# A small matmul moved next to its use, and two pieces of attention spaced evenly, in a kernel of attention and a Fourier mixer

## The chip, the core and the metric

The kernel runs on one core of a Trainium2 chip. Its engines work side by side, each in the order of its own instruction list: TensorE (PE, matmuls into PSUM; its weight loads are shown as PEld), VectorE (DVE), ScalarE (ACT), GpSimd (POOL), and SyncE (SP), which issues nearly all DMA transfers here. Engines wait for one another by semaphores. The metric is the device time of one execution in microseconds (us).

## The reference, cut

```python
q, k, v: (4, 8, 768, 64)            # batch, heads, tokens, head size
# attention: a window of +-16 tokens, and 24 blocks of 32 tokens as extra keys
k_sum = k.reshape(B, H, nb, block, D).max(axis=3)
v_sum = v.reshape(B, H, nb, block, D).mean(axis=3)
scores_l = scale * q @ k.T           # masked to |pos_i - pos_j| < 16
scores_s = scale * q @ k_sum.T + np.log(block)
a = softmax(concat[scores_l, scores_s])
x = a @ concat[v, v_sum]             # then (B, S, H*D) = (4, 768, 512)
# mixer
u  = x + np.real(fft(fft(x, axis=1), axis=2))
un = (u - mean(u)) / sqrt(var(u) + 1e-6)
out = u + relu(un @ w_ch1) @ w_ch2   # 512 -> 2048 -> 512
```

A block's log(32) and mean make a sum: the weight exp(score) times the sum of the block's 32 rows of v. The kernel therefore uses block *sums* of v and a count of 32.

## The kernel before

Four batches go through a pipeline. The dense work of batch b (two layers, 512 to 2048 to 512, each split in halves and done by seven products in place of eight) runs on TensorE together with the attention of batch b+1. Two Python generators are advanced side by side: `gen_hidden` and `gen_out` yield after every product or two, `gen_attention` after every small piece, and `drive` at the end of `_main_program` mixes them at a fixed ratio. For the attention of batches 2 and 3 it is 80 steps of attention on 44 of dense work. What is emitted between two yields is handed to a scheduler together; it sets each engine's order by its own model. So the number of yields between two pieces of attention sets how much dense work lies between them.

A batch's eight heads are four pairs g = 0..3. For a pair of batches 1 to 3:

- `prepare(b, g)` makes kt and qt, the transposed k and q, and km, the block maxima of k. In batches 2 and 3 (past pair 0 of batch 2) DVE transposes (line 693, `STREAM_TRANSPOSE`), in the rest PE does.
- `scores` (lines 773 and 779): 48 small products into two PSUM banks, exp on ACT into p, a multiplication by the mask near on DVE. `sum_scores` (lines 789 and 790): the scores of the blocks, exp into pm.
- `block_sums(b, gg)` fetches the v rows of four heads in four pieces of 192 KB and adds them up on POOL (line 570) to vbs, once for pairs 0 and 1 and once for pairs 2 and 3.
- `scale_sums` (lines 795 and 798) is the block sums' product: PE multiplies vbs with a 0/1 table that spreads the sums over the partitions, and two ACT copies (in batch 1 one DVE operation) write them, masked by half_of, into the single tile vs.
- `values` (lines 811 and 816): 48 products of p with the near values vw, then six of pm with vs, into the same two banks (av); a reciprocal (line 820) and a multiplication on DVE write x.
- `load` fetches q and k of the pair three ahead, `load_values` the near values vw, of the next pair.

The attention's PSUM banks are four in turn, the dense work's another four. In the hidden layer, slice j has seven groups of two matmuls in the order hx, hy, hx, hz, hx, hz, hx (line 1316); a matmul in fp32 shows as two records in the profile. Between the products that use one bank, ACT copies it (lines 1327, 1333, 1335 and 1346) or DVE adds it (line 567). Line 1385 has the products of the output layer (ox, oy, oz).

In `gen_attention` before, a pair of batches 2 and 3 goes: scores, three yields, k's transposition for the next pair, `scale_sums`, two yields, q's transposition, `load`, two yields, `values` and `load_values`, three yields, and the next pair's scores. That is seven steps from scores to values and three from values to scores.

## Time and profile before

| what | us |
|---|---|
| median of three runs | 809.16 (806.12 to 811.9) |
| the profiled execution | 806.47 |
| its span, first to last instruction | 804.5 |
| ACT busy in the span | 229.0 |
| stage with batch 2's attention (282.17 to 382.79): length | 100.62 |
| the same, PE busy | 95.95 |
| the near products of a pair, start to start of its second part (305.81 to 306.94) | 1.13 |

The profile covers one execution; times in it are counted from its first instruction. "PE busy" joins the modelled ends of pipelined matmuls. PEclk is the share of TensorE's full clock that was granted. A row of the timeline gives start, duration, engine, line, operation, the tiles written and read, the shapes and the count, and in brackets the engine's idle time before it with what ended it. Line numbers are those of the kernel before.

### The profile page before, as it was taken

How to read it: one execution, taken by the hardware profiler on the slowest of the kernel's cores; microseconds unless marked ns; L12 is line 12 of the kernel's file. 1: busy time of each engine (PE TensorE's matmuls, PEld its weight loads, DVE VectorE, ACT ScalarE, POOL GpSimd, SP SyncE). 2: the span in 40 equal slices, each digit the busy share in tenths (PEclk: the TensorE clock that was granted, in tenths of full speed). 3: DMA queues.
4: the chain of work that ended last, by engine and by line, in shares of the span. 5: the costliest groups of instructions: out<-in, count | busy, mean ns of one | idle time of the engine just before them, and what ended most of it. 6: DMA issues, size and time to landing. Idle time of an engine off the chain costs nothing.

```text
span 804.5 us, 14469 instructions
## 1 busy us (share of the span) xinstructions
PE 777.9 (97%) x5914; PEld 564.7 (70%) x5914; DVE 494.8 (62%) x1115; ACT 229.0 (28%) x509; POOL 61.7 (8%) x103
## 2 busy tenths in 40 slices
PE   8988999999999979999999999999999999999997
PEld 6776655445589846688669865688669875786586
DVE  5789998797988526653576635563476722532352
ACT  3544656336535122200126112200126102001200
POOL 0012030000000020200120010300030000000000
PEclk9989999999999999999999999999999999999999
DMA  9999597696855279965353159620514143205001
GB/s 228 202 271 193 148 311 187 196 311 204 231 159 141 51 198 237 238 89 133 120 191 138 53 185 185 175 90 11 228 42 152 40 176 144 86 0 229 0 28 55
DMA packets 133354, 121.83 MB, mean 151 GB/s; under 512 B 94464, under 2 KB 114912, under 8 KB 133088
## 3 DMA queue, kind: packets, MB, share of 16 engines
q1 hardware_dynamic: 132016, 118.53, 53.3%
q0 software_dynamic: 576, 2.10, 0.7%
q8 instruction: 48, 0.79, 0.4%
q10 hardware_dynamic: 688, 0.20, 0.1%
q14 instruction: 26, 0.21, 0.1%
HBM read 97.22 MB, written 23.59 MB: 150 GB/s over the span
## 4 chain that ended last, share of the span: by engine, by line
PE 81%; DVE 11%; DMA 3%; ACT 3%; POOL 1%; issue 1%; SPq 0%; ACTq 0%; POOLq 0%; DVEq 0%
PE ox L1385 18%; PE hx L1316 17%; PE oz L1385 9%; PE hz L1316 8%; PE oy L1385 5%; PE o L1362 4%; PE hy L1316 4%; PE y L1212 4%; PE mx L1171 2%; DMA vb<-in_v_dram 2%; DVE w L567 2%; PE av L811 1%; PE unt L1290 1%; PE sc L773 1%; DVE x L567 1%; PE av L816 1%
## 5 line engine op out<-in xcount | busy, mean ns | idle before, releaser
L1316 PE MATMUL hx<-u,w 128*128 128x384 f32 x512 | 187.0, 493 | 4.2 <-DVE h L567 2.9
L1316 PEld LDWEIGHTS hx<-u,w 128*128 128x128 f32 x512 | 95.0, 190 | 72.0 <-DVE h L567 5.3
L1316 PE MATMUL hz<-u,w 128*128 128x384 f32 x256 | 93.3, 486 | 0.0
L1385 PE MATMUL oz<-w,s 128*128 128x256 f32 x336 | 81.1, 379 | 0.0
L1385 PE MATMUL ox<-w,s 128*128 128x256 f32 x336 | 80.3, 380 | 0.0
L1385 PE MATMUL ox<-w,h 128*128 128x256 f32 x336 | 80.2, 381 | 0.0
L567 DVE TENSOR_TENSOR x<-ox,x 128x256 f32<-128x256 f32 x84 | 35.3, 422 | 67.6 <-PE ox L1385 67.4
L1316 PEld LDWEIGHTS hz<-u,w 128*128 128x128 f32 x256 | 48.5, 190 | 34.3 <-ACT h L1335 1.2
L1327 ACT COPY h<-hx 128x384 f32<-128x384 f32 x32 | 15.3, 478 | 199.8 <-PE hx L1316 199.8
L1385 PEld LDWEIGHTS ox<-w,h 128*128 128x128 f32 x336 | 62.9, 190 | 10.4 <-issue 0.6
L1385 PEld LDWEIGHTS ox<-w,s 128*128 128x128 f32 x336 | 63.0, 190 | 9.3 <-DVE x L567 0.8
L1385 PEld LDWEIGHTS oz<-w,s 128*128 128x128 f32 x336 | 63.4, 190 | 8.5
L567 DVE TENSOR_TENSOR h<-hy,h 128x384 f32<-128x384 f32 x32 | 17.8, 555 | 55.9 <-PE hy L1316 55.8
L1316 PE MATMUL hy<-u,w 128*128 128x384 f32 x128 | 47.4, 494 | 0.0
L567 DVE TENSOR_TENSOR h<-hx,h 128x384 f32<-128x384 f32 x32 | 17.7, 555 | 47.3 <-PE hx L1316 46.5
L1362 PE MATMUL o<-w,h 128*128 128x512 f32 x96 | 42.2, 596 | 0.7 <-DVE w L567 0.7
L1346 ACT ACTIVATE h<-hx 128x384 f32<-128x384 f32 x32 | 15.7, 491 | 86.5 <-PE hx L1316 86.4
L1385 PE MATMUL oy<-w,h 128*128 128x256 f32 x168 | 40.1, 380 | 0.0
L1316 PEld LDWEIGHTS hy<-u,w 128*128 128x128 f32 x128 | 24.8, 194 | 17.4 <-issue 1.2
L570 POOL TENSOR_TENSOR vb<-vb 96x512 f32<-96x512 f32 (+2 forms) x24 | 23.6, 984 | 174.6 <-PE hz L1316 66.2
L567 DVE TENSOR_TENSOR x<-oz,x 128x256 f32<-128x256 f32 x42 | 17.7, 422 | 29.7 <-PE oz L1385 29.4
L1385 PEld LDWEIGHTS oy<-w,h 128*128 128x128 f32 x168 | 31.8, 190 | 4.4
(164 smaller groups left out, 1093.8 us busy)
## 6 DMA issues: line engine op xcount, KB each, us to landing
w<-dw SPq DMA_DIRECT2D x44, 896.0 KB, 5.6
words<-in_moe_w_ch_dram SPq DMA_DIRECT2D x32, 512.0 KB, 5.1
dw<-w SPq DMA_DIRECT2D x12, 896.0 KB, 7.1
vw<-in_v_dram SPq DMA_DIRECT2D x47, 192.0 KB, 5.4
out_dram<-x SPq DMA_DIRECT2D x23, 256.0 KB, 2.0
vb<-in_v_dram SPq DMA_DIRECT2D x24, 192.0 KB, 6.3
kn<-in_k_dram SPq DMA_DIRECT2D x9, 384.0 KB, 5.2
qn<-in_q_dram SPq DMA_DIRECT2D x9, 384.0 KB, 6.7
```

The costliest lines, as they stand in the source:

```text
L567: return nc.vector.tensor_tensor(out=out, in0=in0, in1=in1, op=op).ins
L570: nc.gpsimd.tensor_tensor(out=out, in0=in0, in1=in1, op=op)
L773: nc.tensor.matmul(ps[h][r:r + 64, i, :], kt[rows, o:o + 64], qt[rows, o:o + BLOCK], start=True, stop=True)
L811: nc.tensor.matmul(av[r][32 * j:32 * (j + 1), t, :], p[rows, h, i - NB2 * h, :], vw[rows, i, :], start=(t == 0), stop=False, skip_group_ch ...
L816: nc.tensor.matmul(av[r][:, t:t + HT + 1:HT, :], pm[rows, P * t:P * (t + 1)], vs[rows], start=False, stop=(t == HT - 1), skip_group_check= ...
L1171: nc.tensor.matmul(out, y[:, g], table, start=False, stop=True, skip_group_check=True)
L1212: nc.tensor.matmul(y, fgs[b][par][:, st, P * g:P * (g + 1)], fs[par][:, g % 2, st, :], start=(st == 0), stop=(st == n - 1))
L1316: ins = nc.tensor.matmul(ps, w[:, a, kk, :], u[:, r, kk, :], start=start and kk == 0, stop=stop and kk == 1, skip_group_check=True)
L1327: nc.scalar.copy(out=c11, in_=X)
L1346: nc.scalar.activation(out=c21, in_=X, func=AF.Relu)
L1362: nc.tensor.matmul(ps, h[:, n, hf, P * t:P * (t + 1)], wt[2, b, j][:, 2 * hf:2 * hf + 2, :], start=(n, hf) == (0, 0), stop=(n, hf) == (NC ...
L1385: nc.tensor.matmul(ps, left[a][:, n, :], wt[2, b, j][:, r, :], start=start and n == 0, stop=stop and n == NC - 1, skip_group_check=True)
```

## The change

In batches 2 and 3 `scale_sums` is no longer called behind the next pair's k transposition, but just before `values` of its own pair. There are two yields fewer between scores and values and two more between values and the next scores: five and five. As the yields between scores and `prepare` go from three to one, the transpositions of the next pair and the fetches of the pair three ahead are emitted two steps earlier. In batch 1 nothing changes.

```diff
             if held:
+                if b > 1:
+                    scale_sums(b, g - 1)
                 values(b, g - 1, *held, x)
                 if n1 and b > 1:
                     load_values(*n1)
...
             elif held:
-                yield
-                if b > 1:
-                    yield
+                for _ in range(5 if b > 1 else 1):
                     yield
             if g < NP:
                 held = scores(b, g)
...
             yield
             if g == NP:
                 return
-            if b > 1:
-                yield
-                yield
             if n1:
                 prepare(*n1, *((1,) if b > 1 else ()))
-            scale_sums(b, g)
+            if b == 1:
+                scale_sums(b, g)
             if b > 1:
                 yield
                 yield
```

## The prediction

> **What bounds the kernel now.** I read the page's first two parts first: is one engine the bound, and where is it not busy?

> ```profile
> PE 777.9 (97%) x5914; PEld 564.7 (70%) x5914; DVE 494.8 (62%) x1115; ACT 229.0 (28%) x509; POOL 61.7 (8%) x103
> PEclk9989999999999999999999999999999999999999
> ```

> TensorE (PE) is the bound. The change moves work and removes none, so it can win only PE's idle time, and what idle time costs in clock. So next the table of waits, PE alone, between 230 and 720 us, which holds all of batches 2 and 3:

> ```profile
> PE vs L795 <- POOL vbs L570: 5.5, 2, 4.7
> PE hx L1316 <- DVE h L567: 0.7, 1, 0.7
> ```

> In 490 us PE waits three times for long: twice for the block sums that line 795 multiplies (4.67 us in batch 2, 0.83 in batch 3), once for VectorE (DVE). The chain of waits shows what ends the long one:

> ```profile
> 285.20 8.84 DMA vb<-in_v_dram
> 294.04 0.02 issue
> ...
> 298.17 0.32 POOL vbs L570
> 298.50 0.04 issue
> 298.54 0.43 PE vs L795 x2
> 298.97 0.38 PE hx L1316
> ```

> The last quarter of the raw block rows lands at 294.04, GpSimd (POOL) adds it up by 298.49, and the product can start at 298.54. PE reached it at 293.87. Third, the windows around it; the columns are the stretch, its length, PE busy, weight loads, DVE, ACT, POOL, granted clock, DMA share, GB/s:

> ```profile
> 77.41:80.82 3.41, 1.02 (x23) 0.63 (x21) 3.27 (x13) 3.32 (x8) 0.00 (x0) 1.00 1.02 323
> 80.82:84.23 3.41, 3.29 (x50) 2.96 (x55) 2.04 (x4) 2.67 (x6) 0.00 (x0) 0.50 0.22 77
> 292.45:295.86 3.41, 1.42 (x5) 0.54 (x3) 2.55 (x4) 0.49 (x1) 2.88 (x3) 1.00 0.44 145
> 295.86:299.28 3.42, 0.74 (x4) 0.61 (x5) 0.00 (x0) 0.27 (x2) 2.39 (x4) 1.00 0.00 0
> 299.28:302.69 3.41, 3.41 (x7) 1.82 (x6) 0.00 (x0) 0.73 (x3) 0.94 (x1) 0.50 0.87 227
> ```

> After the wait the clock is halved for 3.41 us: matmul work of 1.7 us takes 3.4. The wait in batch 2 thus costs 4.67 + 1.70 = 6.4 us, the largest removable item behind 230 us.

> **The change, part by part.** The orders of both programs on each engine can be compared without running them.

> *1. The product of the block sums moves back.* Before, PE's order in batches 2 and 3 is: hx of slice 0 (end), vs, hx, hy, hx, hz of slice 1, values. After: hx (end), hx, hy of slice 1, vs, values. (As the values come earlier too, the product gains two groups of matmuls, not four.) In the timeline four such matmul records take 1.29 us start to start, so vs is reached 2 x 1.29 = 2.58 us later, at 293.87 + 2.58 = 296.45. Those two groups wait for nothing late: slice 1 of the weights was fetched long before, and hy's bank is freed by an ACT copy that ends at 294.40. The block sums' fetches and sums lie ahead of everything moved, on SP's queue and on POOL, so their end stays at 298.49 at best. The wait becomes 298.54 - 296.45 = 2.09 us.

> One thing can move that end: DVE now runs qt's transposition and the slice's first addition during POOL's sums. In batch 3, where DVE was at work beside them, the four large sums took 4.26 us instead of 3.92, and DVE paid more:

> ```profile
> 478.86 3.21 DVE L567 TENSOR_TENSOR p<-p,near 128x384 f32<-128x384 f32 x2 [3.61 <-ACT p L779]
> 480.26 4.26 POOL L570 TENSOR_TENSOR vb<-vb 96x512 f32<-96x512 f32 x4 [0.15 <-DMA vb<-in_v_dram]
> ```

> The pair of multiplications by near took 1.03 us in batch 2. [...] The rows would add up to 0.34. I take 0.2 of it, as the last three sums alone are met. Batch 2 gains 2.58 - 0.2 = 2.4 us.

> *2. The clock.* [...] The windows show 0.74 and 1.02 busy followed by half clock, and 1.42 not. With 2.2 us idle, a window is busy 1.2 at the least, and only if the wait lies in one window whole, (3.41 - 2.2)/3.41 = 0.35 of the phases. I take the full 1.70, ends 0 and 1.70.

> *3. Batch 3's wait.* PE is at the product at 484.14, the sums are there at 484.93. After, PE comes at about 486.7: 0.83 us are gone. The 0.73 us of hx on DVE lie before anything moved and stay.

> *4. What the product now delays.* From vs to the values' last part it is a new, short chain: vs, two ACT copies into the vs tile, then the pm times vs products. Before, a whole group or more lay between.

> ```profile
> 338.15 0.33 PE L795 MATMUL vs<-vbs,sel 96*128 96x64 f32 x2
> 338.32 1.08 PE L1385 MATMUL ox<-w,h 128*128 128x256 f32 x4
> 338.58 0.52 ACT L798 ACTIVATE vs<-vs,half 128x64 f32<-128x64 f32 x2 [0.60 <-PE vs L795]
> ```

> The copies end 338.58 + 0.52 - 338.15 = 0.95 us after the product starts. PE issues on after 0.17 us, the 48 near products need 1.13 (av at 305.81, its second part at 306.94), so the first product that reads vs comes after 1.30. The cover is 0.35 us, cost nothing, if ACT is free. In batch 3's third pair ACT still has the h copy of 0.49 us behind the last hx and ends at about 1.24: covered barely. Ends: 0, and 0.2 x 8 = 1.6 us.

> *5. Values and scores spaced five and five.* Ten steps per pair before (7 + 3), ten after (5 + 5): the period and the scores stay, the values come two steps earlier, about one group. They need p multiplied by near, 290.6 in batch 2, six us before. The next scores have more room for the banks. Cost: nothing.

> *6. The transpositions* (two of 0.97 us and a reduction of 0.94 per pair, DVE) go two steps earlier. What DVE must not be late for is the addition between the third and the fourth hx product, whose cover is the hz group, 1.29 us; in the new order the transpositions stand before the slice's first addition or behind its last, some 2 us clear of it. In the third pair of batch 2 the five s sums and the values' arithmetic (3.1 + 1.3 us) stand before ox's first addition; it then ends some 0.1 us before PE wants the bank. Ends 0 and 0.3, value 0.

> *7. SP's queue.* The eight fetches of the pair after next (k and q, 96 KB each) go ahead of one 896 KB weight slice, and the values' four fetches ahead of a store. The slice, issued at 299.83 before, then goes out at about 309.9, where the last q fetch ended; DMA engines are busy from 300 to 325. The longest landing of such a slice there is 8.2 us, so 318; hx of slice 3, at 327.0 before, comes at about 322. Spare 4 us: cost nothing. The stores are read a batch later. The later half of the block sums stays on POOL at 326.6 against its product at about 333.

> Sum: -2.4 - 1.70 - 0.83 = -4.9 us. The profiled execution took 806.47 (span 804.5 and 2.0 around it), so 801.6. Its time lies 2.7 us under the median of the three runs, 809.16; carried to that, 804.3.

> **The rivals.** (a) *The clock still halves.* [...] Against: 1.2 busy at the least lies over 1.02. Gain 3.2: 806.0. (b) *The wait goes whole*, because sums end earlier, or runs over the median hide longer waits that this change shortens as well. All of PE's waits here plus clock make 4.67 + 1.70 + 0.83 + 0.73 = 7.9: 801.2 at the most. For it: runs reach 811.9. Against: nothing moved stands ahead of the sums. (c) *Slower: the copies are exposed.* If the values' near products do not cover them (the wait is held at the head of the group), each of eight pairs pays 0.95 + 0.1 - 0.17, about 0.9: 7 us, net +2.1, 811.3. It decides from 4.9/8 = 0.6 us per pair. Against: the wait stands on the first product that reads vs, not on the first near product. (d) *Nothing comes of it*: the saved time is lost at the next late thing (a weight slice, ox's addition): 809. Against: 4 us spare, and PE idle nowhere else.

> **How the numbers follow.** Main case 0.55 at 804.3, own range 801.5 to 807; (a) 0.20; (b) 0.12; (c) 0.07; (d) 0.06. The three runs spread over 5.8 us, so a median moves by some 2 us by itself; 1% (8.1 us) is about what can be told from no change. Range 799.5 to 809.5: it takes in (a), (b) and (d), and leaves out most of (c). Faster by over 1%, below 801.1: half of (b) and a low draw of the main case, 0.17. Slower by over 1%, above 817.2: 0.04, an unforeseen wait. Within: 0.79.

> **What would show it.** Right: PE's wait on vbs in batch 2 near 2.1 us and none in batch 3, no half-clock window behind it, av's second part 1.1 us behind its first in all eight pairs. Wrong: a PE wait on ACT's vs copies at line 816, a wait of hx on a weight slice's DMA, ox waiting on DVE in the third pair, or vbs after 299.

## The result, and the profile after

| | before | after |
|---|---|---|
| median, us | 808.88 (806.12 to 811.9, 9 runs) | 804.49 (801.24 to 805.53, 9 runs) |
| profiled execution (span) | 806.47 (804.5) | 802.52 (799.9) |
| stage with batch 2's attention, start to start of slice 0's hx | 100.62 | 95.79 |
| stage with batch 3's attention | 94.42 | 92.13 |

The ratio of after to before is 0.9938, with a 95% interval of 0.9917 to 0.9958: 4.4 us less, against 4.9 forecast. Line numbers from 1009 on are two lower than before.

The page of the changed kernel, its first two parts (busy time by engine, granted clock):

```profile
PE 776.3 (97%) x5914; PEld 566.0 (71%) x5914; DVE 497.7 (62%) x1115; ACT 228.8 (29%) x509; POOL 62.0 (8%) x103
...
PEclk9989999999999999999999999999999999999999
```

PE is as busy as it was and has as many instructions; only idle time could go. The waits of PE from 230 to 720 us:

```profile
PE vs L795 <- POOL vbs L570: 1.6, 1, 1.6
PE unt L1288 <- DVE x L567: 0.3, 2, 0.2
```

5.5 us in two waits for the block sums have become 1.6 in one. Batch 3's wait is gone, and so is hx's wait of 0.7 us for DVE, which comes back in other profiles (step 3 below). The timeline of the changed kernel around the product (start, duration, engine, line, operation, tiles, shapes, count, idle time before it and its releaser):

```profile
294.74 5.17 POOL L570 TENSOR_TENSOR vb<-vb 96x512 f32<-96x512 f32 x5 [65.80 <-DVE h L1320]
...
299.99 0.47 POOL L570 TENSOR_TENSOR vbs<-vb 96x64 f32<-96x64 f32 x1
...
300.51 0.43 PE L795 MATMUL vs<-vbs,sel 96*128 96x64 f32 x2 [1.59 <-POOL vbs L570]
...
300.87 1.20 PE L811 MATMUL av<-vw,p 64*32 64x65 f32 x96
300.98 0.52 ACT L798 ACTIVATE vs<-vs,half 128x64 f32<-128x64 f32 x2 [2.84 <-PE vs L795]
...
302.00 0.94 PE L816 MATMUL av<-vs,p 64*128 64x130 f32 x12
```

PE comes to the product at 300.51 - 1.59 = 298.92, 14.29 us after its stage began at 284.63; before it was 293.87 - 282.17 = 11.70. The sums still end late. The vs copies end at 301.50, half a microsecond before the first product that reads them, and the second part of av starts 1.13 us behind the first: no wait there. In each of the fourteen traces all half-clock stretches away from the end of the program last 3.41, 6.83 or 10.24 us and start on one grid, so the windows here are cut on that grid, 3.41 us each. Those around the wait (stretch, length, PE, PEld, DVE, ACT and POOL busy, granted clock, DMA share, GB/s):

```profile
297.45:300.86 3.41, 1.82 (x7) 0.87 (x5) 3.22 (x7) 0.48 (x1) 2.77 (x4) 1.00 0.01 5
300.86:304.28 3.42, 3.42 (x114) 2.67 (x114) 2.40 (x8) 0.52 (x2) 0.42 (x1) 1.00 0.77 197
```

The second row shows the full clock behind the wait, where before the row read 0.50. In batch 3 the product doesn't wait at all:

```profile
482.49 0.31 POOL L570 TENSOR_TENSOR vbs<-vb 96x64 f32<-96x64 f32 x1
...
483.21 0.33 PE L795 MATMUL vs<-vbs,sel 96*128 96x64 f32 x2
```

The profile leaves a question. The two stages are 4.83 and 2.29 us shorter, 7.1 together, and the median gains only 4.4. In this one execution batch 2's stage began 2.5 us later than in that of before, in code that the change doesn't touch. Is that chance, or was the profiled execution a lucky one behind 284 us?

### The profile page after: what moved, and what is told of

The parts are those of the page before. It is cut to its first block, busy times and chain, and to the rows that moved or that the text cites. A ratio compares the mean times of both kernels' runs of the same rounds, so it can differ in the third digit from the quotient of the medians.

```text
span 799.9 us, 14473 instructions
## 1 busy us (share of the span) xinstructions
PE 776.3 (97%) x5914; PEld 566.0 (71%) x5914; DVE 497.7 (62%) x1115; ACT 228.8 (29%) x509; POOL 62.0 (8%) x103
## 4 chain that ended last, share of the span: by engine, by line
PE 83%; DVE 11%; ACT 2%; DMA 1%; issue 1%; POOL 1%; ACTq 0%; DVEq 0%; POOLq 0%
PE ox L1383 18%; PE hx L1314 18%; PE oz L1383 9%; PE hz L1314 9%; PE oy L1383 5%; PE o L1360 4%; PE hy L1314 4%; PE y L1210 4%; PE mx L1169 2%; DVE w L567 2%; PE sc L773 2%; PE av L811 1%; PE unt L1288 1%; DVE x L567 1%; PE av L816 1%; DVE words L1066 1%
## 5 line engine op out<-in xcount | busy, mean ns | idle before, releaser
L567 DVE TENSOR_TENSOR x<-ox,x 128x256 f32<-128x256 f32 x84 | 35.3, 423 | 68.0 <-PE ox L1383 67.7
L567 DVE TENSOR_TENSOR h<-hx,h 128x384 f32<-128x384 f32 x32 | 17.8, 556 | 53.6 <-PE hx L1314 52.9
L567 DVE TENSOR_TENSOR h<-hy,h 128x384 f32<-128x384 f32 x32 | 17.7, 555 | 42.8 <-PE hy L1314 42.6
L570 POOL TENSOR_TENSOR vb<-vb 96x512 f32<-96x512 f32 (+2 forms) x24 | 23.7, 989 | 174.4 <-ACT p L779 66.5
L567 DVE TENSOR_TENSOR x<-oz,x 128x256 f32<-128x256 f32 x42 | 17.7, 422 | 30.4 <-PE oz L1383 30.2
```

The costliest lines, as they stand in the source:

```text
L567: return nc.vector.tensor_tensor(out=out, in0=in0, in1=in1, op=op).ins
L570: nc.gpsimd.tensor_tensor(out=out, in0=in0, in1=in1, op=op)
```

## The experiments

All kernels compute the whole result. W is my theory: *what counts is PE's wait for the block sums, and the half clock that it brings*. Ratios are to the kernel before on the same chip (medians 807.77 in the first group of four, 809.83 in the second).

### One half of the change at a time

*x1_product: the product alone at the values, spacing seven and three.*

```diff
             if held:
+                if b > 1:
+                    scale_sums(b, g - 1)
                 values(b, g - 1, *held, x)
...
-            scale_sums(b, g)
+            if b == 1:
+                scale_sums(b, g)
```

> The product alone at the values; the spacing stays seven and three. On TensorE the product then stands four groups of matmuls (5.2 us) later than before, not two. Theory W (the gain is TensorE's wait for the block sums and the half-clock window behind it): in batch 2 no wait at all and no half-clock window, in batch 3 none; 4.67 + 1.70 + 0.83 = 7.2 us less than before, about 801.7 against 808.9, ratio 0.991, faster than the changed kernel by 1.6 to 2.3 us. Rival S (the gain comes from the earlier transpositions, fetches and values of the even spacing): no gain, about 809.

Measured: 800.33 us, ratio 0.9904 (0.9877 to 0.9932): 7.4 us less, where the whole change gains 4.4. In the table of waits of PE, from 230 to 720 us, the block sums are missing, and there is a new first line:

```profile
PE sc L773 <- issue: 1.0, 1, 1.0
PE hx L1319 <- DVE h L567: 0.6, 1, 0.6
```

The sums are ready at 299.43, and PE comes to the product at 300.61, 16.70 us into the stage: with seven steps ahead of it, it stands four groups later than before, not two. The intervals of this ratio and of the change's overlap a little, so the lead of 3 us over the change is likely and not certain; x8 and x6 below have the same ratio as x1.

*x2_spacing: the spacing of five and five alone, the product still behind k's transposition.*

```diff
             elif held:
-                yield
-                if b > 1:
-                    yield
+                for _ in range(5 if b > 1 else 1):
                     yield
...
-            if b > 1:
-                yield
-                yield
             if n1:
```

> The spacing alone, five and five; the product stays where it was in the program, behind the next pair's k transposition, which now comes two steps earlier. On TensorE the product then stands one group (1.29 us) earlier than before. Theory W: the wait in batch 2 grows to about 6 us with a half-clock window or two behind it, in batch 3 to about 2.1; 2.6 us or more slower than before, about 811.5, ratio 1.003. Rival S: it has all of the gain, about 804.5, ratio 0.994.

Measured: 813.13, ratio 1.0069 (1.0042 to 1.0097). This half of the change costs 5.4 us, because it pulls the product one group ahead (PE comes to it 10.42 us into the stage, 11.70 before). The waits and the windows of this kernel:

```profile
PE vs L795 <- POOL vbs L570: 9.0, 2, 6.1
```

```profile
291.09:294.50 3.41, 1.20 (x4) 0.38 (x2) 3.04 (x6) 0.00 (x0) 1.77 (x2) 1.00 0.85 241
294.50:297.92 3.42, 0.00 (x0) 0.00 (x0) 1.33 (x2) 0.00 (x0) 3.18 (x4) 0.50 0.05 17
297.92:301.33 3.41, 2.96 (x6) 1.94 (x7) 0.00 (x0) 0.52 (x2) 0.31 (x1) 0.50 0.47 142
301.33:304.75 3.42, 3.42 (x7) 1.72 (x6) 0.00 (x0) 0.92 (x2) 1.26 (x1) 0.50 1.30 178
482.24:485.65 3.41, 2.13 (x7) 0.95 (x5) 3.38 (x4) 0.00 (x0) 3.03 (x4) 1.00 1.01 406
485.65:489.06 3.41, 1.72 (x7) 1.19 (x8) 3.41 (x6) 0.52 (x2) 1.48 (x3) 1.00 0.29 75
```

In batch 2 the wait is 6.07 us and three windows run at half clock, two of them with work in them: (2.96 + 3.42) / 2 = 3.19 us lost besides. In batch 3 PE waits 2.97 us (the last two rows), spread over two windows, and the clock stays.

*x4_batch2: the whole change, in batch 2 only.*

```diff
-                yield
-                if b > 1:
-                    yield
+                for _ in range((1, 5, 3)[b - 1]):
                     yield
...
+                if b == 2:
+                    scale_sums(b, g - 1)
...
```

> The whole change in batch 2 alone; batch 3 as before. Theory W: most of the gain, 2.6 of the wait and 1.7 of the clock, about 4.2 us, 804.7, ratio 0.995; in batch 3 the wait of about 0.8 us for the block sums is there. Rival S: half of the gain, about 806.7.

Measured: 805.15, ratio 0.9969 (0.9943 to 0.9996). Batch 3's stage is that of before, 94.42 us, with its wait of 0.82; batch 2's is 96.27, close to that of the whole change. By the stages 4.35 of the change's 7.1 us are batch 2's, by the medians 2.6 of 4.4; the interval is too wide to tell the share closer.

### Is the vs chain covered?

*x3_pm_first: the change, with the pm times vs products ahead of the 48 near products, so that they come right behind the product.*

```diff
...
+        for part in (block_part, near_part) if b > 1 else (near_part, block_part):
+            part()
```

> The changed kernel with the six pm times vs products ahead of the 48 near products in batches 2 and 3, so that the near products no longer cover ScalarE's copies of vs; the order left to the scheduler puts half a group (0.65 us) between the product and them. Theory W with the copies at 0.95 us from the product's start: 0.2 to 0.3 us of wait per pair at line 816's place, 8 pairs, 1.6 to 2.4 us over the changed kernel, about 806.5. Rival C (the copies were exposed already in the changed kernel): about the same as the changed kernel, 804.5, and a wait of the same size in both.

Measured: 804.53, ratio 0.996 (0.9934 to 0.9986), no slower than the change. The expected 1.6 to 2.4 us didn't come: in seven of eight pairs other dense products were placed between. In the eighth (batch 3's last) nothing was, and the timeline shows what the chain costs bare:

```profile
526.51 0.33 PE L795 MATMUL vs<-vbs,sel 96*128 96x64 f32 x2
526.94 0.52 ACT L798 ACTIVATE vs<-vs,half 128x64 f32<-128x64 f32 x2 [1.20 <-PE vs L795]
...
527.52 0.94 PE L819 MATMUL av<-vs,p 64*128 64x130 f32 x12 [0.67 <-ACT vs L798]
```

So 0.67 us is the price without cover, in the one pair that shows it. The change itself has no wait for the copies in any pair, and there the near products stand between.

### The wait from the other side, and the place apart from the spacing

*x6_early_sums: the kernel before; only the fetches of the block rows of pairs 0 and 1 aren't held back behind the dense layer's first loads.*

```diff
-            with tc.issue_after(marks["load"]):
-                block_sums(b, 0)
+            block_sums(b, 0)
```

> The order of the kernel before, product behind k's transposition, seven and three; only the fetches of the block rows for pairs 0 and 1 are issued without being placed behind the dense layer's first weight loads. Theory W (the wait for the sums, with the half clock it brings, is what the change takes away; any remedy of the wait gives the same): the rows land earlier, the wait of 4.67 us in batch 2 falls under 2, the wait of 0.83 in batch 3 goes, no window at half clock behind them; 803 to 805, ratio near 0.994. Rival T (the gain comes from where the product stands among the matmuls, not from its wait): the wait shrinks and the time stays within 1 us of before, ratio 0.999 to 1.002. If the weights that now come behind these fetches are late, hx or hy waits for a DMA and the time is over before.

Measured: 800.64, ratio 0.9908 (0.9885 to 0.9931). That is more than the 803 to 805 expected. PE's order around the two products that waited is that of before; further on the scheduler placed some products otherwise (the third pair's vs of batch 2 stands ahead of the last hx, not between two ox). T falls. POOL's timeline and PE's chain (start, duration, what):

```profile
275.26 5.17 POOL L570 TENSOR_TENSOR vb<-vb 96x512 f32<-96x512 f32 x5 [50.06 <-DMA vb<-in_v_dram]
280.50 0.32 POOL L570 TENSOR_TENSOR vbs<-vb 96x64 f32<-96x64 f32 x1
```

```profile
291.28 1.29 PE hx L1315 x4
292.57 0.17 PE vs L795 x2
292.74 1.34 PE hx L1315 x4
```

The sums are ready 12 us ahead of their product, and no weight slice is late for it: PE's only new wait is one of 0.9 us of ox for DVE at 445.9, outside both stages. The two stages take 94.81 and 92.12 us, 186.93 together. Batch 3's has no wait at all, hx's for DVE included. One line on the supply side gives more than the change, and about as much as x1.

*x7_later: the product at the place that it has in the changed kernel, spacing seven and three.*

```diff
-            scale_sums(b, g)
+            if b == 1:
+                scale_sums(b, g)
             if b > 1:
                 yield
                 yield
+                scale_sums(b, g)
```

> Product at the place that it has in the changed kernel (about two groups later than before), but spacing seven and three as before. Theory W: a wait of 1.6 to 2.1 us in batch 2, none in batch 3, no half clock; same time as the changed kernel, 804 to 805, ratio 0.993 to 0.996. Rival S' (the spacing of five and five costs by itself, so the product alone at this place is better): 801 to 802, ratio under 0.992, though the wait is 1.6 or more.

Measured: 804.21, ratio 0.9938 (0.9912 to 0.9965): the ratio of the change. S' isn't borne out. The profile has a wait of 1.2 us for the sums and full clock, but also two stops of sc with no releaser, 2.7 us together (below), so it isn't a clean copy of the changed kernel's.

*x8_early_prep: x1, with the next pair's transpositions and the fetches two steps earlier.*

```diff
-            if b > 1:
-                yield
-                yield
             if n1:
...
-            if b > 1:
+            for _ in range(3 if b > 1 else 0):
```

> The kernel with the product alone moved to the values (seven and three), and besides the next pair's transpositions and the fetches of the pair three ahead two steps earlier, as the change puts them. Theory W: neither costs anything, as DVE and SP's queue have room; no wait for the sums, same time as the product alone, 800 to 801, ratio 0.990 to 0.991. Rival P (the earlier transpositions and fetches are what the change loses against the product alone): 803 to 805, with a wait on DVE or on a weight slice in the table of waits.

Measured: 801.34, ratio 0.9906 (0.9871 to 0.9941): that of x1. P isn't borne out; the earlier transpositions and fetches cost nothing that can be seen.

*x5_one_ahead: the product one step ahead of the values, seven and three.*

```diff
-            scale_sums(b, g)
+            if b == 1:
+                scale_sums(b, g)
             if b > 1:
...
+                scale_sums(b, g)
```

The added call is the last but one step of a round of the loop; the values follow one step later.

> Product one step (about one group or less) ahead of the values, seven and three: a whole piece of dense work lies between it and the values, so the copies have more cover than in any version at the values. Theory W: no wait for the sums and the copies cost nothing in either, so as the product alone at the values, 800 to 801.5. Rival C (the copies at the values cost a part of the gain, though no wait shows it): faster than the product alone at the values by 1 us or more.

Measured: 802.91, ratio 0.992 (0.9885 to 0.9955), a little over the 800 to 801.5 expected. No wait for the sums. C isn't borne out, as the run is no faster than x1, but the test is weaker than planned: in five of the eight pairs the scheduler put the product right ahead of the values again, and only three have dense work between them. The profile, of the slowest of its seven executions, shows a stop of sc (the score products) of 1.45 us, and behind it a window at half clock.

### Does the wait vary from execution to execution?

Four more profiles, of kernels profiled above, one execution each, for the question that the first one left.

> The changed kernel once more, unchanged, for a second profiled execution. Theory V (the wait for the sums varies from execution to execution with the landing of the rows, and the first profile happened to be a good one: its median gains less than its stages did): the wait in batch 2 differs from 1.59 by 0.5 us or more, up to 3, perhaps with a half clock behind it, and batch 2's stage is 94.2 us plus the waits plus the half clock. Rival F (the wait is fixed, the stage too, and the rest varies before batch 2): 1.4 to 1.8 us and a stage of 95.5 to 96.1.

> As the run before it: a third profiled execution of the changed kernel. V: the wait for the sums differs from the other two by 0.5 us or more. F: 1.4 to 1.8 us.

> The kernel before once more, for a second profiled execution. V: its wait in batch 2 varies too, between 3.5 and 6 us, and its stage is 94.2 us plus the waits plus the half clock; with a wait of 5.5 or more, two or three windows at half clock instead of one. F: 4.5 to 4.9, one window.

> The product alone moved to the values, once more. V and F: its place leaves it some 2.6 us behind that of the changed kernel, so no wait for the sums in batch 2, or one under 0.5; stage of batch 2 between 94.2 and 95.5. If it waits for more than 1 us, its lead over the changed kernel isn't due to the wait.

| | wait for sums, batch 2 | at half clock behind it | batch 2's stage | time |
|---|---|---|---|---|
| r1_after | 2.16 | none | 96.84 | 806.44 |
| r2_after | 1.59 | one window | 98.14 | 806.51 |
| r3_before | 4.76 | two windows | 101.75 | 812.88 |
| r4_product | 0 | none | 95.23 | 802.89 |

V holds in part: the wait itself moves by some half a microsecond in one of two cases (r2_after's 1.59 is what F said of the wait, but F's stage of 95.5 to 96.1 us fits neither run), and the clock behind it comes and goes. r2_after is the row that decides. Its product and the two windows, to be put beside those of the first profile of after:

```profile
301.19 0.43 PE L795 MATMUL vs<-vbs,sel 96*128 96x64 f32 x2 [1.59 <-POOL vbs L570]
```

```profile
299.40:302.81 3.41, 1.82 (x101) 1.46 (x102) 2.96 (x8) 0.52 (x2) 1.57 (x3) 1.00 0.15 49
302.81:306.23 3.42, 3.42 (x15) 2.32 (x16) 1.29 (x4) 0.00 (x0) 0.93 (x1) 0.50 1.07 202
```

The same wait, the same 1.82 us of busy PE in the window, and this time the clock halves: 1.71 us. What differs is where the window's edge falls: there five of its seven records are dense products, here nearly all of the 101 are the small products of the values. And in r3_before the wait of 4.76 us lay so that one window was empty:

```profile
298.94:302.35 3.41, 0.00 (x0) 0.00 (x0) 1.28 (x3) 0.44 (x1) 3.15 (x4) 1.00 0.16 59
302.35:305.77 3.42, 2.16 (x5) 1.56 (x6) 0.00 (x0) 0.52 (x2) 1.05 (x3) 0.50 0.31 104
305.77:309.18 3.41, 3.41 (x6) 1.73 (x6) 0.00 (x0) 0.48 (x1) 1.26 (x1) 0.50 0.96 262
```

That costs (2.16 + 3.41) / 2 = 2.79 us of clock, not 1.70.

### One account for all fourteen profiles

The length of batch 2's stage, less the waits for the sums, less the stops of sc, less half of the PE time in half-clock windows:

| profile | stage | sums | sc | clock | rest |
|---|---|---|---|---|---|
| before | 100.62 | 4.67 | 0 | 1.70 | 94.25 |
| r3_before | 101.75 | 4.76 | 0 | 2.79 | 94.20 |
| after | 95.79 | 1.59 | 0 | 0 | 94.20 |
| r1_after | 96.84 | 2.16 | 0.29 | 0 | 94.39 |
| r2_after | 98.14 | 1.59 | 0.53 | 1.71 | 94.31 |
| x4_batch2 | 96.27 | 1.60 | 0.27 | 0 | 94.40 |
| x7_later | 98.68 | 1.19 | 2.71 | 0 | 94.78 |
| x3_pm_first | 95.05 | 0.39 | 0.93 | 0 | 93.73 |
| x1_product | 95.14 | 0 | 1.05 | 0 | 94.09 |
| r4_product | 95.23 | 0 | 1.15 | 0 | 94.08 |
| x8_early_prep | 95.14 | 0 | 1.09 | 0 | 94.05 |
| x5_one_ahead | 97.47 | 0 | 1.45 | 1.70 | 94.32 |
| x6_early_sums | 94.81 | 0 | 0.58 | 0 | 94.23 |
| x2_spacing | 103.41 | 6.07 | 0 | 3.19 | 94.15 |

What is left is 93.7 to 94.8 us in all of them, whatever the order, the spacing and the place of the product. That PE's time is busy time plus waits is bookkeeping; what the table adds is that half of the work in half-clock windows is the right price, and that no order costs PE more than about half a microsecond of other time. It also answers the question of the first profile. Batch 2's stage began at 282.17 and at 287.15 us in the two profiles of before, so a shift of 2.5 us there needs no cause in the change. Both stages together take 187.92, 189.84 and 191.03 us in the three profiles of after (mean 189.6), 195.04 and 196.40 in the two of before (195.7): 6.1 us apart, where the first pair of profiles showed 7.1. The first profile of after had the shortest stages of its three. x1's two profiles, 188.09 and 188.36, lie 7.5 us under before, and its median gains 7.4; x6's 186.93 lies 8.8 under, and its median gains 9.2. The 1.7 us between after's 6.1 and its median's 4.4 stay open; the interval of the ratio runs from 3.4 to 6.7 us, so the two don't contradict each other.

## Why the prediction was right, point by point

The mechanism is borne out: a later product waits less (change, x1), an earlier one more (x2), and the same wait taken away from the supply side gains as much (x6). The sizes came out with some luck. By the means of the profiles batch 2's wait fell by 2.9 us (2.4 forecast), batch 3's by 1.4 (0.83 forecast; r3_before waits 2.06) and the clock's loss by 1.7 (1.70 forecast). That is 6 us, and the median fell by 4.4, closer to the 4.9 forecast than the parts are.

*Step 1, the product's place.* Two groups, 2.58 us, were forecast; PE comes 14.29 - 11.70 = 2.59 us later in its stage. The wait that is left was put at 2.3 us with the slip of the sums; it measured 1.59, 2.16 and 1.59. What I took for an end fixed at 298.49 moves: counted from the stage's start, the sums end at 16.3 and 16.4 us in the profiles of before and at 15.8, 16.4 and 15.8 in those of after. The slip on POOL is there (the last sum took 0.47 us instead of 0.32), but smaller than that spread. The sign of being wrong "vbs after 299" did come by the trace's time (300.46), as the stage began 2.46 us later; counted from its start the sums were not late.

*Step 2, the clock.* I took the full 1.70 us. That a window with 1.2 us of busy PE keeps the clock was my estimate, from two windows of before that lost it (0.74 and 1.02 us busy) and one that kept it (1.42), and I gave 0.20 to rival (a), that it halves all the same. The runs show both: full clock in two profiles of after, half in one. Waits of 1.59 (r2_after) and 1.45 us (x5) were followed by half clock, as was one of 2.11 with shorter ones beside it (before, ending at 80.94); one of 2.97 (x2, batch 3) was not. So in these runs neither a wait's length nor PE's busy share alone told it, and 1.2 us was too low a bar: x2's window of 1.20 lost its clock. Taking 1.70 before and 0 after as fixed was the weak term of the sum, and no run shows it as fixed. It measured 1.70 and 2.79 us in the two profiles of before, mean 2.25, and 0, 0 and 1.71 in the three of after, mean 0.57. That the difference, 1.68, is the forecast figure again is luck: two errors of about half a microsecond cancel.

*Step 3, batch 3.* Its wait is gone in all three profiles of after. That hx's 0.73 us wait for DVE "stays" was wrong as a statement: it is missing in the first profile of after, 0.6 in r1_after and 0.5 in r2_after, and missing in r3_before. It goes with the moment at which POOL's sums meet DVE's multiplications by near, and not with this change: in the two profiles without it POOL's first sum starts 0.02 us behind the first multiplication, which then takes 0.56 us; in the three with it the sum starts 0.01 to 0.22 us ahead, and the multiplication takes 1.46 to 1.67.

*Step 4, the copies.* No exposure, as costed. The cover was put at 0.35 us; the timeline shows 0.50 in batch 2's first pair. Without cover the one pair that shows it pays 0.67 (x3), under the 0.9 of rival (c).

*Steps 5 and 6, spacing and transpositions at nothing.* x8 beside x1, and x7 beside the change, bear this out. But "spacing: nothing" holds only for the values and scores. Alone, the spacing moves the product forward and costs 5.4 us (x2); step 1 had that netted ("two groups, not four") without saying what it means: that half of the change works against the other.

*Step 7, SP's queue.* The weight slice was issued at 308.00 and landed at 313.87, some 9 us ahead of its hx; the forecast was 318.

*Rival (b)*, the wait gone whole at 801.2 at the most, is not what the change does. It is what x1 and x6 do, at 800.3 and 800.6 (7.4 and 9.2 us under before in their groups).

## What to carry to other kernels

Where PE waits for one small product's operand, count in groups of matmuls how far each part of an edit moves it: here one part moved it four groups back (x1) and the other took two of them away again. Before moving the consumer look at who holds the producer back: taking one ordering constraint off a fetch (x6) gave as much as the best move. And a stall that is left at some 2 us isn't safe because one profile shows the full clock behind it: here the price was 1.7 us or nothing from one execution to the next, so the version with no stall is the better aim.

## What the hardware showed that I had not expected

```profile
73.15:76.56 3.41, 1.34 (x12) 1.10 (x11) 3.41 (x20) 2.13 (x6) 0.33 (x2) 1.00 0.98 190
76.56:79.97 3.41, 2.98 (x14) 2.95 (x14) 3.10 (x11) 2.75 (x6) 0.00 (x0) 0.50 1.09 302
```

Windows of mostly small products (64 columns or fewer) didn't keep to that. r2_after's lost the clock with 1.82 us busy; x5's with 1.96, while x1's kept it with 2.37:

```profile
327.22:330.63 3.41, 1.96 (x98) 1.61 (x96) 1.73 (x2) 0.00 (x0) 2.52 (x2) 1.00 0.99 401
330.63:334.04 3.41, 3.41 (x23) 1.45 (x16) 1.29 (x2) 1.36 (x3) 2.81 (x5) 0.50 1.12 328
323.56:326.98 3.42, 2.37 (x105) 1.77 (x104) 0.96 (x3) 0.56 (x2) 3.18 (x4) 1.00 0.99 407
326.98:330.39 3.41, 3.41 (x14) 2.01 (x11) 1.11 (x2) 1.63 (x4) 1.40 (x4) 1.00 0.91 211
```

Why x1's kept it and the other two lost it is not shown: no run varied the small products of a window by themselves.

*PE stops in the middle of sc, with no releaser.* Ten of the fourteen profiles, those with little or no wait for the sums, show a new stop of 0.3 to 1.5 us in the scores, mostly around 325 us. In x1's timeline:

```profile
323.51 1.06 PE L773 MATMUL sc<-qt,kt 64*64 64x32 f32 x57
325.61 0.78 PE L773 MATMUL sc<-qt,kt 64*64 64x32 f32 x39 [1.05 <-issue]
```

The trace's packets show a transfer of 16 KB on an instruction queue just before each: the DMA view of x1, 323.05 to 324.1 us, has it as

```profile
q1 hardware_dynamic: 62, 0.41, 98.3%
q8 instruction: 1, 0.02, 6.1%
```

In all eleven stops (x7 has two) PE goes on 1.42 to 1.61 us after such a transfer ended, while data transfers kept the DMA engines nearly full (in ten of the eleven, with 98.3% in x1; 0.75 in one of x7's). Whether the transfer makes PE stop is not shown: no experiment varied it, and such transfers also pass without a stop, as the profile of before has six between 280 and 345 us. Neither profile of before, nor x2's, nor the first of after has a stop in this stage, and why not is open as well. It is what is late next: x1 has it for 1.05 and 1.15 us in its two profiles.
